# Block-product operands summed in place from twelve staged parts, with a retimed spectral chain, in a gated spectral/GEGLU kernel

## The chip, the cores and the metric

The kernel runs on one core of one Trainium2 chip. The metric is the device time of one execution in microseconds; a profiled execution also gives its span, from the first instruction to the last, which is a little shorter.

## The reference, cut to what matters

```python
x = A_x                                        # [1, 2048, 576], float32
g = sigmoid((x * gate_w).sum(-1, keepdims=True))
X = rfft2(x, axes=(-2, -1)) * (w_r + 1j * w_i) # 2048 x 289 complex filter
a = irfft2(X, s=(2048, 576), axes=(-2, -1))
h = gelu(B_x @ w_gate) * (B_x @ w_up)          # 576 -> 4608, tanh form of gelu
b = h @ w_down                                 # 4608 -> 576
return g * a + (1 - g) * b
```

`B_x` has the same values as `x`. Two unequal halves: a gated feed-forward network, nearly all of the arithmetic, and a two-dimensional FFT filter.

## The kernel before, in words

**Matrix work (TensorE, PE).** Operands are kept as two reduced-precision pieces, high and low, so that a float32 product is three matmuls (high·high, low·high, high·low). The 4608 hidden features are 36 blocks of 128; two blocks for one half of the tokens (1024, as two groups of 512) are a *pair*. There are 36 pairs, q = 0 to 35, the first 18 for one token half, the rest for the other. `PLAN` (L33) says for each pair how its gate and up projections are made:

- `c`, `conv` (L1248): plain chains, 8 of 14 matmuls of 512 columns, 112 in all (`chain`, L755).
- `s`, `products` (L1048): a block-product scheme in which seven products of quarter blocks stand for eight, 7 times 2 times 7 = 98 matmuls (`seven`, L1035). It needs seven operands of x: the quarters a11, a12, a22 and four sums s1 to s4 of the quarters, and as many of the weights, made on ScalarE (ACT) and VectorE (DVE) by `prep_b` and `total`.

The plan before is 2 c, 10 s, 11 c, 13 s. So block products run in two stages, each opened by `operands(p)` (L941), which makes the seven operands of that token half. The quarters come from memory as three feature parts of four quarters each (`load_xs`, L937: two parts before the stage, the third into the place of the first once it is used). Per part: four sums on DVE (L962), copies to the high pieces on ACT (`copy`, L214), differences to the low pieces on DVE (L974), and for the third, packed part the same three steps for seven operands (`tail_of`, L916). They are written to `sx`, which shares its place with the spectral tile buffer `til`, and s4 to `gu[2]`, one of three weight buffers that `conv` rotates through. `operands` waits until the pair before the stage has begun (L954).

Behind each pair stand 8 down projections (`down`, L850), each 12 matmuls of 288 columns, an eviction on ACT (L860) and an accumulating DMA on the POOL queue (L848). `pop` takes them from a list; the first pair of a block-product stage has only 4 to take, at the products that `downs` (L1080) names.

**Spectral work (DVE, ACT, a little PE).** One generator, `spectral` (L600), issues it in a fixed order: operands of stage one; forward FFT along rows for each token half (`forward_rows`); a wait for the first c pair after stage one (`until(2)`); then row-to-tile copies (`into_tiles`, `moved`, L500), the token-axis stages (`first_tiles`; `columns`, L232, with 192 matmuls of 290 columns, the filter, and small DMAs that swap corners between partitions; `last_tiles`), tile-to-row copies (`into_rows`); operands of stage two; and, once stage two has begun (`until(3)`), the inverse FFT along rows and the adds into the output.

**What orders the work.** Everything is laid out when the program is built; each engine then runs its own instructions in that order and waits on semaphores. After every few matmuls the program calls `gap()` (L656). A gap runs timed jobs (`at`), one job of the list `aux`, and then steps of the spectral generator while a *credit* is above zero. `tick` (L648) adds RATE times the matmuls' nominal time, every DVE job of the matrix part subtracts its nominal cost, and every step of the generator subtracts what it yields. A yield of `None` ends the turn until the next gap. At the gap the credit is cut to at most 1.2. In `columns` each of six steps per block of 128 points charges 5.45/6 and yields `None` (L371). Should the operands not be done when stage two is due, L1288 to L1290 force gaps with no matmul between them until they are.

In both stages x for the second token half is reloaded by `reload_x` (L1242) through three staging places, one feature block in every second gap, around pairs 17 and 18.

Of the kernel before, what the change touches and what calls it, by code (L numbers as in the profile page):

```python
# [13 lines left out]
ALU = mybir.AluOpType  # L14
# [15 lines left out]
RATE = 1.0  # L30
STEP = 6
PAIRS = NT // 2
PLAN = "c" * 2 + "s" * 10 + "c" * 11 + "s" * 13  # L33
# [126 lines left out]
def _build(nc, tc, a):  # L160
    with ExitStack() as ctx:
# [70 lines left out]
        def columns():  # L232
# [77 lines left out]
            for kb in range(18):  # L310
# [18 lines left out]
                for g in range(STEP):  # L329
# [41 lines left out]
                    credit[0] -= 5.45 / STEP if on else 0.0  # L371
# [128 lines left out]
        def moved(at):  # L500

            yield None
            for t in range(8):
                for c in range(2):
                    o, i = at(t, c)
                    if c:
                        vec.tensor_tensor(o, i, sgn, ALU.mult)
# [92 lines left out]
        def spectral(rows):  # L600
            yield from operands(0)
# [314 lines left out]
        def tail_of(o, x):  # L916

            copy(o, x)
            yield 0.0
            vec.tensor_tensor(o, x, f(o), ALU.subtract)  # L920
            yield 0.72
            for q in (0, 64):
                copy(o[q:q + 32], x[q:q + 32])
            yield 0.0

        def tails_of(pairs):

            work = [tail_of(*p) for p in pairs]
            for _ in range(3):
                for w in work:  # L930
                    yield next(w)
                yield None
# [4 lines left out]
        def load_xs(p, i):  # L937
            for q in range(4):
                nc.sync.dma_start(parts_of[i % 2][q], a["xs"][p, q // 2, q % 2][:, i])

        def operands(p):  # L941
# [5 lines left out]
            tails = [sx[:, 6144 + TB * i:6144 + TB * (i + 1)] for i in range(6)] + [s4[:, 2048:2560]]  # L947
# [5 lines left out]
            m = out_rows[3][:, 0:TB]  # L953
            while current[0] < starts[p] - 1:  # L954
                yield None
            for i in range(3):
                a11, a12, a21, a22 = parts_of[i % 2]
                if i == 2:
                    yield from tails_of([(ops[n][2], x) for n, x in (("a11", a11), ("a12", a12), ("a22", a22))])
                for o, x, z, op in ((m, a21, a22, ALU.add), (a21, a11, a21, ALU.subtract),  # L960
                                    (a11, m, a11, ALU.subtract), (a12, a12, a11, ALU.subtract)):
                    vec.tensor_tensor(o, x, z, op)  # L962
                    yield 0.72
                sums = (("s1", m), ("s2", a11), ("s3", a21), ("s4", a12))
                yield None
                if i == 2:
                    yield from tails_of([(ops[n][2], x) for n, x in sums])
                else:
                    for n, x in sums:
                        copy(ops[n][0][:, i], x)  # L970
                    yield None
                    yield None
                    for n, x in sums:
                        vec.tensor_tensor(ops[n][1][:, i], x, f(ops[n][0][:, i]), ALU.subtract)  # L974
                        yield 0.61
                if i == 0:
                    load_xs(p, 2)
# [70 lines left out]
        def products(q):  # L1048
# [31 lines left out]
            downs = (1, 1, 1, 1, 0, 0, 0) if q in starts else (0, 1, 1, 1, 2, 1, 2)  # L1080
# [4 lines left out]
            for n, (name, nd) in enumerate(zip(("a11", "a12", "s2", "s1", "s3", "s4", "a22"), downs)):  # L1085
# [19 lines left out]
                if then == "c":  # L1105
# [4 lines left out]
                    elif n == 5:  # L1110
                        prep_gu(q + 1, 0)
                    elif n == 6:
                        at(2, lambda: prep_gu(q + 1, 1))
# [46 lines left out]
        gu_of, where = {}, [gu[2], gu[0], gu[1]]  # L1160
        for q, m in enumerate(PLAN):
            if m == "s":
# [7 lines left out]
                where, base = [w[k // 2], gu[2], w[1 - k // 2]], 2 * (q + n)  # L1170
# [55 lines left out]
        aux.append(lambda: [load_d(1), load_xs(0, 0), load_xs(0, 1)])  # L1226
# [10 lines left out]
        def load_x(i):  # L1237
            if i < 2 * KT:
                tb, k = divmod(i, KT)
                nc.sync.dma_start(xst[i % 3], a["xt"][1][:, k, tb * TB:(tb + 1) * TB])  # L1240

        def reload_x(tb):  # L1242
            for k in range(KT):
                i = KT * tb + k
                aux.append(lambda i=i, k=k: [prep_x(tb, k, xst[i % 3]), load_x(i + 3)])
                aux.append(lambda: None)
# [111 lines left out]
```

## Time and profile before

| | |
|---|---|
| time, median of 3 runs | 1376.36 us (1374.35 to 1376.40) |
| the profiled execution | 1374.25 us, span 1372.5 us |
| PE busy | 1344.1 us (98% of the span), 7364 matmuls |
| weight loads busy | 1186.9 us (86%) |
| DVE busy | 1142.8 us (83%), 1605 instructions |
| ACT busy | 846.9 us (62%), 1444 instructions |
| POOL busy | 263.2 us (19%) |
| DMA | 227.42 MB, mean 166 GB/s |

A busy share is a mean over stages: PE is busy nearly throughout, and DVE is far busier in the block-product stages than in the c stage. Matmuls are pipelined, so a record of 0.39 us does not say how often one can start; the distance between two starts does. The stretches that follow are named by microseconds from the start of the span: c pairs until 79, stage one of block products until 429, c pairs with the spectral tiles and columns until 887, stage two until the end.

### The profile page before, as it was taken

The page shows a single profiled execution, that of the slowest core. Times are in us where ns is not written, and L with a number is a line of the kernel's source. Part 1 is how long each engine was busy: PE and PEld are TensorE (multiplying, and loading weights), DVE is VectorE, ACT ScalarE, POOL GpSimd, SP SyncE. Part 2 cuts the span into 40 slices and gives each one's busy share as a digit, 9 for nine tenths or more (in the row PEclk, how much of TensorE's full clock was granted, in tenths as well). Part 3 has the DMA queues.
Part 4 walks back from the last instruction along what each step waited for, and adds up shares of the span by engine and source line. Part 5 has one row for each costly group of instructions (what it writes and reads, how often), then busy time and mean ns, then how long its engine had stood idle before and what let it go on. Part 6 is the DMA issues. An engine that isn't in the chain of part 4 may idle for free.

```text
span 1372.5 us, 20070 instructions
## 1 busy us (share of the span) xinstructions
PE 1344.1 (98%) x7364; PEld 1186.9 (86%) x7364; DVE 1142.8 (83%) x1605; ACT 846.9 (62%) x1444; POOL 263.2 (19%) x322
## 2 busy tenths in 40 slices
PE   9998999999999999999999999889999999999998
PEld 7887888888889888889888988767888888888888
DVE  7689999989999768867786587689989779989854
ACT  5585676666674455465665544676676776676682
POOL 0011122221122222122210111211222232222231
PEclk9999999999999999999999999989999999999999
DMA  9465776696667877799987657744666797667797
GB/s 332 163 128 146 148 142 131 130 272 129 126 110 147 195 139 148 181 236 236 265 233 222 132 109 206 173 98 103 130 132 129 134 266 131 135 116 137 138 220 181
DMA packets 102770, 227.42 MB, mean 166 GB/s; under 512 B 12432, under 2 KB 22672, under 8 KB 101776
## 3 DMA queue, kind: packets, MB, share of 16 engines
q0 software_dynamic: 44928, 90.98, 44.1%
q1 hardware_dynamic: 57744, 135.17, 29.7%
q8 instruction: 57, 0.93, 0.3%
q14 instruction: 41, 0.34, 0.1%
HBM read 121.70 MB, written 97.26 MB: 160 GB/s over the span
## 4 chain that ended last, share of the span: by engine, by line
PE 85%; DVE 6%; ACT 4%; DMA 2%; issue 2%; SPq 0%; DVEq 0%; ACTq 0%
PE pdn L835 30%; PE pgu L1041 5%; PE pgu L1043 5%; PE pgu L1042 5%; PE pone L1041 5%; PE pgu L760 5%; PE pgu L762 5%; PE pgu L761 4%; PE pone L1043 4%; PE pone L1042 4%; PE pgu L1044 2%; PE pone L1044 2%; PE pone L760 2%; PE pone L762 2%; PE pone L761 2%
## 5 line engine op out<-in xcount | busy, mean ns | idle before, releaser
L848 POOL DMA_DIRECT2D yd<-stg x264 | 228.9, 868 | 994.2 <-ACT stg L860 861.2
L860 ACT ACTIVATE stg<-pdn,omg 128x576 f32<-128x576 f32 x276 | 203.9, 739 | 278.7 <-PE pdn L835 274.1
L835 PE MATMUL pdn<-dn,hb 128*128 128x288 f32 x2556 | 371.2, 295 | 2.5 <-DVE hb L1065 1.3
L835 PEld LDWEIGHTS pdn<-dn,hb 128*128 128x128 f32 x2556 | 357.8, 189 | 14.3 <-DVE hb L1065 1.8
L214 ACT ACTIVATE gu<-wq 64x256 fp32r<-64x256 f32 (+4 forms) x353 | 228.5, 666 | 101.7 <-DVE gu L1006 90.9
L1006 DVE TENSOR_TENSOR gu<-wq,gu 128x768 fp32r<-128x768 f32 x161 | 153.5, 953 | 18.9 <-ACT gu L214 18.5
L835 PE MATMUL pdn<-dn,hx 128*128 128x288 f32 x876 | 134.2, 295 | 0.2 <-DVE wq L899 0.2
L835 PEld LDWEIGHTS pdn<-dn,hx 128*128 128x128 f32 x876 | 124.9, 189 | 4.1 <-DVE wq L899 0.5
L760 PE MATMUL pgu<-xhi,gu 128*128 128x512 f32 x300 | 117.9, 393 | 0.0
L762 PE MATMUL pgu<-xlo,gu 128*128 128x512 f32 x300 | 117.8, 393 | 0.0
L761 PE MATMUL pgu<-xhi,gu 128*128 128x512 f32 x300 | 117.7, 392 | 0.0
L1023 DVE TENSOR_TENSOR wq<-wq 128x768 f32<-128x768 f32 x92 | 87.7, 953 | 7.9 <-ACT gu L214 7.9
L214 ACT ACTIVATE hb<-gl 128x512 fp32r<-128x512 f32 x66 | 41.4, 627 | 51.4 <-DVE gl L817 51.4
L762 PEld LDWEIGHTS pgu<-xlo,gu 128*128 128x128 f32 x300 | 56.6, 189 | 12.3
L760 PEld LDWEIGHTS pgu<-xhi,gu 128*128 128x128 f32 x300 | 56.8, 189 | 9.9
L761 PEld LDWEIGHTS pgu<-xhi,gu 128*128 128x128 f32 x300 | 56.7, 189 | 9.9
L1044 PE MATMUL pgu<-sx,gu 128*128 128x512 f32 x138 | 54.5, 395 | 6.6 <-ACT sx L214 6.6
L739 DVE TENSOR_TENSOR dn<-wq,dn 128x576 fp32r<-128x576 f32 x72 | 54.2, 753 | 5.0 <-ACT dn L214 5.0
L1041 PE MATMUL pgu<-xhi,gu 128*128 128x512 f32 x140 | 55.6, 397 | 2.5 <-DVE xraw L1077 2.4
L1041 PE MATMUL pgu<-sx,gu 128*128 128x512 f32 x140 | 55.7, 398 | 1.9 <-ACT gl L214 1.9
L1041 PE MATMUL pone<-xhi,gu 128*128 128x512 f32 x136 | 53.5, 394 | 3.7 <-DVE xraw L1077 3.7
L1043 PE MATMUL pgu<-sx,gu 128*128 128x512 f32 x140 | 55.2, 395 | 0.0
(243 smaller groups left out, 2871.2 us busy)
## 6 DMA issues: line engine op xcount, KB each, us to landing
yd<-stg POOLq DMA_DIRECT2D x264, 288.0 KB, 4.9
wq<-ws SPq DMA_DIRECT2D x92, 384.0 KB, 4.2
wq<-wd SPq DMA_DIRECT2D x72, 288.0 KB, 4.6
wq<-wgu SPq DMA_DIRECT2D x24, 640.0 KB, 5.8
colm<-col POOLq DMA_DIRECT2D x32, 256.0 KB, 6.3
tmp<-wf SPq DMA_DIRECT2D x16, 290.0 KB, 5.1
hx<-til SPq DMA_DIRECT2D x64, 72.5 KB, 5.0
til<-hx SPq DMA_DIRECT2D x64, 72.5 KB, 3.7
```

What stands on the lines that cost most here:

```text
L214: act.activation(o, i, AF.Copy)
L760: pe.matmul(ps, w[:, 0, k, c], xhi[tb][:, k], start=k == 0, stop=False)
L761: pe.matmul(ps, w[:, 1, k, c], xhi[tb][:, k], start=False, stop=False)
L762: pe.matmul(ps, w[:, 0, k, c], xlo[tb][:, k], start=False, stop=False)
L835: pe.matmul(ps[half], h[:, l, c], d[:, k, half * HD:(half + 1) * HD], start=part == 0 and n == 0, stop=part == 1 and n == 2)
L848: pl.dma_start(yd[u], o, accum_op=ALU.add)
L860: put(u, lambda o: act.activation(o.rearrange("p (c k) -> p c k", c=2), v[:, :, 0:HD], AF.Copy, scale=omg[:, u:u + 1]), i == 0)
L1006: vec.tensor_tensor(o, x.rearrange("p (c k) -> p c k", c=3), f(w[:, 256:1024]).rearrange("p (c k) -> p c k", c=3), ALU.subtract)
L1041: pe.matmul(ps, hi, xh[:, t], start=start and t == 0, stop=False, skip_group_check=True)
L1042: pe.matmul(ps, lo, xh[:, t], start=False, stop=False, skip_group_check=True)
L1043: pe.matmul(ps, hi, xl[:, t], start=False, stop=False, skip_group_check=True)
L1044: pe.matmul(ps, tl, xt, start=False, stop=stop, skip_group_check=True)
```

## The change

In words, by part:

1. `PLAN` is 2 c, 10 s, 10 c, 14 s: pair 22 becomes a block-product pair, and stage two begins one pair sooner.
2. `RATE` 1.0 to 1.03; the cap on the credit 1.2 to 1.4; a step of `columns` charges 4.9/6 in place of 5.45/6.
3. `moved` yields `None` after every second tile in place of every tile.
4. `operands`: all three parts (twelve quarters) have staging places of their own, loaded together: for stage one by the generator's first step (before: eight of them earlier, by an `aux` job at about 25 us), for stage two right after `columns` (before: after `last_tiles`). The sum s1 is written over a22 and not into a separate place; sums charge 0.61 in place of 0.72. Order: the tails of a11, a12, a22 come first, s1 to s3 before s4, copies on ACT one or two per yield; only the last part waits for the pair before the stage.
5. Weight buffers: which of the three `conv` uses when is turned so that `gu[2]` is free one pair before the stage whatever the number of c pairs, and `prep_gu` of the first c pair after a stage is retimed to match (`early`).
6. The first pair of a stage takes its four down projections at products 3, 5, 6 and 7 in place of 1 to 4.
7. `reload_x` starts with the last feature block and uses gaps 0, 2, 4, 6, 10 of eleven.

```diff
-RATE = 1.0
+RATE = 1.03
-PLAN = "c" * 2 + "s" * 10 + "c" * 11 + "s" * 13
+PLAN = "c"*2+"s"*10+"c"*10+"s"*14
...
-                    credit[0] -= 5.45 / STEP if on else 0.0
+                    credit[0] -= 4.9 / STEP if on else 0.0
...
                     else:
                         copy(o, i)
-                yield None
+                if t % 2:
+                    yield None
...
         def spectral(rows):
+            load_xs(0)
+            for _ in range(3):
+                yield None
             yield from operands(0)
...
             cols[0] = False
+            load_xs(1)
             yield from last_tiles()
-            load_xs(1, 0)
-            load_xs(1, 1)
             yield from into_rows(1)
...
-            credit[0] = min(credit[0], 1.2)
+            credit[0] = min(credit[0], 1.4)
...
         parts_of = [[xraw[:, q] for q in range(4)],
-                    [tmp[:, 1536:2048], tmp[:, 2048:2560], misc[:, 0:TB], misc[:, SW:SW + TB]]]
+                    [tmp[:, 1536:2048], tmp[:, 2048:2560], misc[:, 0:TB], misc[:, SW:SW + TB]],
+                    [tmp[:, 0:512], tmp[:, 512:1024], tmp[:, 1024:1536], out_rows[3][:, 0:TB]]]
...
+            def sums(i):
+                a11, a12, a21, a22 = parts_of[i]
+                for o, x, z, op in ((a22, a21, a22, ALU.add), (a21, a11, a21, ALU.subtract),
+                                    (a11, a22, a11, ALU.subtract), (a12, a12, a11, ALU.subtract)):
                     vec.tensor_tensor(o, x, z, op)
-                    yield 0.72
+                    yield 0.61
+            def steps():
+                raw, most = ("a11", "a12", "a22"), ("s1", "s2", "s3")
+                for n in raw:
+                    high(n, 2)
+                yield from sums(0)
+                for n in most:
+                    high(n, 0)
+                yield from sums(1)
+                for n in raw:
+                    low(n, 2)
+                    quarter(n)
+                    yield 0.61
+                for n in most:
+                    high(n, 1)
+                for n in most:
+                    low(n, 0)
+                    yield 0.61
+                while acts:
+                    yield None
+                yield from sums(2)
+                for n in most:
+                    high(n, 2)
+                for n in most:
+                    low(n, 1)
+                    yield 0.61
+                while acts or current[0] < starts[p] - 1:
+                    yield None
+                for i in range(3):
+                    high("s4", i)
+                for n in most:
+                    low(n, 2)
+                    quarter(n)
+                    yield 0.61
+                while acts:
+                    yield None
+                for i in range(3):
+                    low("s4", i)
+                    yield 0.61
+                quarter("s4")
+                while acts:
+                    yield None
+
+            for v in steps():
+                for _ in range(2 if v is None else 1):
+                    if acts:
+                        acts.pop(0)()
+                yield v
...
-            downs = (1, 1, 1, 1, 0, 0, 0) if q in starts else (0, 1, 1, 1, 2, 1, 2)
+            downs = (0, 0, 1, 0, 1, 1, 1) if q in starts else (0, 1, 1, 1, 2, 1, 2)
...
-                where, base = [w[k // 2], gu[2], w[1 - k // 2]], 2 * (q + n)
+                x, y, base = w[k // 2], w[1 - k // 2], 2 * (q + n)
+                where = ([gu[2], x, y], [x, y, gu[2]], [x, gu[2], y])[c % 3]
+                early[q + n - 1] = c % 3
...
-        aux.append(lambda: [load_d(1), load_xs(0, 0), load_xs(0, 1)])
+        aux.append(lambda: load_d(1))
```

In the new `operands`, `high(n, i)` and `quarter(n)` put ACT copies into the list `acts`, `low(n, i)` issues a DVE difference, and `c` is the number of c pairs that follow the stage.

More of the change, by code (lines that the diff above doesn't have):

```diff
@@ L952, in operands @@
             ops["a22"] = (xhi[1][:, 2:4], xlo[1][:, 2:4], tails[6])
[L953 to L970, printed above, removed]
-                    yield None
-                    yield None
[L973 to L977, printed above, removed]
@@ new lines, in operands, with place_of, high, quarter @@
+            where = {"a11": 0, "a12": 1, "a22": 3, "s1": 3, "s2": 0, "s3": 2, "s4": 1}
+            acts = []
+            def place_of(n, i, l):
+                return ops[n][l][:, i] if i < 2 else ops[n][2]
+            def high(n, i):
+                acts.append(lambda: copy(place_of(n, i, 0), parts_of[i][where[n]]))
+            def quarter(n):
+                for k in (0, 64):
+                    acts.append(lambda k=k: copy(ops[n][2][k:k + 32], parts_of[2][where[n]][k:k + 32]))
+            def low(n, i):
+                x = parts_of[i][where[n]]
+                vec.tensor_tensor(place_of(n, i, 1), x, f(place_of(n, i, 0)), ALU.subtract)
```

45 lines of the change are left out of this document (20 added, 25 removed).

## The prediction

> **What bounds the kernel now.** I read the page first: busy shares, then the chain that ended last.
>
> ```profile
> span 1372.5 us, 20070 instructions
> PE 1344.1 (98%) x7364; PEld 1186.9 (86%) x7364; DVE 1142.8 (83%) x1605; ACT 846.9 (62%) x1444; POOL 263.2 (19%) x322
> ...
> PE 85%; DVE 6%; ACT 4%; DMA 2%; issue 2%; SPq 0%; DVEq 0%; ACTq 0%
> ```
>
> PE bounds the kernel: time goes only with matmuls, or with PE waits. Where those waits lie, the windows show, by stage.
>
> ```profile
> 79.00:125.00 46.00, 41.91 (x206) 34.57 (x205) 41.92 (x65) 32.65 (x58) 4.33 (x6) 0.95 0.52 125
> 160.00:195.00 35.00, 35.00 (x196) 31.05 (x195) 32.96 (x52) 24.11 (x47) 6.90 (x8) 0.95 0.73 146
> 230.00:265.00 35.00, 35.00 (x196) 31.06 (x195) 34.90 (x44) 21.86 (x40) 6.91 (x8) 0.95 0.70 131
> 655.00:702.00 47.00, 44.51 (x251) 39.54 (x249) 35.59 (x58) 30.32 (x54) 11.06 (x16) 0.95 1.03 264
> 870.00:905.00 35.00, 28.32 (x147) 24.39 (x145) 25.63 (x38) 24.26 (x43) 3.48 (x4) 0.86 0.36 75
> 905.00:940.00 35.00, 29.58 (x133) 23.64 (x133) 32.90 (x40) 21.81 (x39) 3.46 (x4) 0.91 0.44 96
> ```
>
> Second column: PE busy, full except at the two openings of block-product stages (79:125, 870:940) and a little in the columns (655:702). To price them I took the first matmul of pairs 2, 3, 4, 5 and of 22, 23, 24, 25, with the matmul before pair 22 and one in pair 23, from the timeline of PE (each from its own short stretch).
>
> ```profile
> 79.20 0.39 PE L1041 MATMUL pone<-xhi,gu 128*128 128x512 f32 x1
> 112.22 0.47 PE L1041 MATMUL pgu<-xhi,gu 128*128 128x512 f32 x1 [0.79 <-DVE xraw L1077]
> 148.40 0.40 PE L1041 MATMUL pone<-xhi,gu 128*128 128x512 f32 x1
> 183.45 0.40 PE L1041 MATMUL pgu<-xhi,gu 128*128 128x512 f32 x1
> 848.40 0.39 PE L767 MATMUL pgu<-xtl,gu 128*128 128x512 f32 x1
> 848.62 0.39 PE L760 MATMUL pgu<-xhi,gu 128*128 128x512 f32 x1
> 886.84 0.39 PE L1041 MATMUL pgu<-xhi,gu 128*128 128x512 f32 x1
> 895.00 0.80 PE L1044 MATMUL pgu<-sx,gu 128*128 128x512 f32 x1 [6.63 <-ACT sx L214]
> 931.29 0.47 PE L1041 MATMUL pone<-xhi,gu 128*128 128x512 f32 x1 [1.11 <-DVE xraw L1077]
> 967.43 0.40 PE L1041 MATMUL pgu<-xhi,gu 128*128 128x512 f32 x1
> ```
>
> A settled block-product pair takes 183.45 - 148.40 = 35.05 us, pair 22 as a c pair 886.84 - 848.62 = 38.22. The pitch at 512 columns is 0.22 to 0.23 us (848.40 to 848.62); 98 of 0.2267 make 22.2, so the 96 narrow ones of a full pair take 12.85. A stage's first pair has 4 down projections in place of 8 and should take 22.2 + 6.4 = 28.6. Stage one: 33.02 and 36.18, lost 4.4 + 1.1 = **5.5 us**. Stage two: 44.45 and 36.14, lost 15.9 + 1.1 = **17.0**. What PE waited for:
>
> ```profile
> PE pgu L1044 <- ACT sx L214: 6.6, 1, 6.6
> PE pone L1041 <- DVE xraw L1077: 3.7, 2, 2.6
> PE pone L276 <- DVE colm L269: 2.8, 1, 2.8
> ```
>
> The longest is the row at 895.00 above, for an operand in sx at the opening of stage two: the operands are late. The others are DVE behind its queue, and one block of the columns. The clock column (0.86, 0.91 against 0.95) says that part of the 17.0 is matmuls run at a lower clock between the waits.
>
> **The change part by part.** *Pair 22 as block products*: 38.22 - 35.05 = **-3.2 us**, 14 wide matmuls fewer. This one is certain.
>
> *Are the operands of stage two in time?* The stage is now due one pair (38 us) sooner. The marks of the spectral chain: pair 12 begins (PE); forward rows are done and the tile copies begin, and later the operands (DVE); the column products from first to last; the operands' last copies (ACT).
>
> ```profile
> 428.82 0.40 PE L760 MATMUL pgu<-xhi,gu 128*128 128x512 f32 x1
> ```
> ```profile
> 452.00 0.71 DVE L507 TENSOR_TENSOR til<-rows,sgn 128x289 f32<-128x289 f32 x1
> 870.67 0.69 DVE L962 TENSOR_TENSOR orow<-xraw 128x512 f32<-128x512 f32 x1
> ```
> ```profile
> L276 PE MATMUL pone<-colm x192: 290/298/404, 565.8 to 780.0; 128*128 128x290 f32 x192
> ```
> ```profile
> 900.92 3.84 ACT L214 ACTIVATE sx<-xraw 32x512 fp32r<-32x512 f32 x6
> ```
>
> The chain ended at 904.8, stage two was due at 886.8: 18 us late. Savings:
> - Forward rows ended 23 us after pair 12 began. A block-product pair earns 98 x 0.2265 + 96 x 0.131 = 34.8 of credit and spends 19.6 on its own DVE jobs (4 x 1.22 + 6 x 0.61 + 11 x 0.88 + 2 x 0.68), leaving 15.2; at RATE 1.03, 16.2, or 7% more. Over some 340 us (452 less pair 2's begin and a reload) that is 22 us. Sooner than pair 12 the chain may not go on: **-22**.
> - Row and tile copies: four passes, four `None` fewer each. A c pair has 24 gaps in 38.22 us, 1.59 each: **-25**. With the copies of `til` waiting for a DMA between two of the passes I keep 20.
> - Columns: 16.5 blocks of six steps, 99 gaps, in 214 us. Less 192 column matmuls at the pitch of the narrow ones (12.85/96 = 0.134), 26 us, and 3 of waits, 185 us hold 116 gaps, so 17 were passed over because credit was below zero. The smaller charge and larger rate save between none and all of them (0 to 27 us): **-10**.
> - The rest of 452 to 871, less 214 of columns and four passes of some 19 each, 130 us, is paced by credit: 3%, **-4**.
> - Operands: the first two thirds now run before the wait; dearest at credit, 12 sums at 0.61 for 0.72: **-1**.
>
> Sum 57, from 904.8 to about 848; due at 848.6 less what stage one gives. So just in time, with perhaps 10 to 20 us to either side. Being slightly late now costs little, since a11, a12, a22 come first and s4, which the sixth product takes, last: the wait of 6.6 at the first product's tail should go. What stays is DVE catching up, as in stage one (5.5). I leave 5 of the 17.0: **-12** (bounds 0, if it is as late as before, and -16).
>
> *Stage one.* The parts are now loaded after the stores of the held tiles, and the tails, from the third part, are the first copies on ACT.
>
> ```profile
> 41.73 2.84 SPq L881 DMA_DIRECT2D yd<-til  x4
> ```
> ```profile
> xraw<-xs SPq DMA_DIRECT2D x16, 256.0 KB, 5.0
> ```
> ```profile
> 47.50 3.18 PE pdn L835 x24
> ...
> 53.88 3.18 PE pdn L835 x24
> ```
> ```profile
> L860 ACT ACTIVATE stg<-pdn,omg 128x576 f32<-128x576 f32 x276 | 203.9, 739 | 278.7 <-PE pdn L835 274.1
> ```
> ```profile
> ACT colm L214 <- DMA til<-hx: 2.8, 1, 2.8
> ```
>
> SP is past those stores at 44.6; twelve issues of 0.5 to 0.7 us (2.84 for four) and 5.0 to land put the last quarter at 56 to 58. In the trace every engine starts its instructions in program order, and the copies stand four gaps after, ahead of the eviction of the second down projection (47.50 to 50.7). PE comes to its fourth at 55.5 and needs that buffer. Three copies of 0.64 (3.84 for six) and an eviction of 0.74 after 56 free it at 58.7: PE waits 3 us (0 if the loads land by 52, 5 if at 58). Queued behind on ACT are gelu and evictions; on DVE the sums wait for part one till about 50, and gated products stand behind them; on SP pair 2's weights stand behind the loads, due 25 us later. **+3**. Against it, ACT's copies are done before the stage and spread one to a yield, and the four projections stand where PE waited for DVE: of the 5.5 I take **-2.5** (+3 to -5: the first weights get 3 us less lead). [...] In the trace of before ACT's longest wait for a DMA is the 2.8 above.
>
> *RATE on DVE.* 3% of 34.8 is 1.04 us more spectral work per block-product pair. The window 230:265 shows DVE busy 34.90 of 35, no room. But two neighbours show that records overlap:
>
> ```profile
> 202.17 1.49 DVE L94 TENSOR_TENSOR rows<-rows 128x1280 f32<-128x1280 f32 x1
> 203.57 0.68 DVE L1077 TENSOR_TENSOR xraw<-xraw,pgu 128x512 f32<-128x512 f32 x1
> ```
>
> The next starts 1.40 after a record of 1.49. With 0.09 hidden in each of 44 to 52 instructions, the room is anywhere from 0 to 4 us per pair. No room costs 1.04 in each of 21 pairs with spectral work, 22 us; full room nothing. I take **+1.5**, nearer to room, since PE waits nowhere at the present load and 160:195 shows 2 us free even by the column. [...]
>
> *Copies two by two.*
>
> ```profile
> L214 ACT ACTIVATE til<-rows 128x289 f32<-128x289 f32 x16 | 11.9, 760 | 0.0
> ```
>
> ACT takes two of these per gap, 1.5 us in 1.59, beside its own work; a backlog of 2 to 3 us per pass, which PE's buffers may just bear: **+0.5** (0 to 3). *Columns*: the waits stay (0, -3 to +5). The sums in place are as many and as wide as before: 0. Stage two's loads move ahead of `last_tiles`: SP holds them till the columns' last DVE jobs free their places, with a c pair's weights behind, which have most of 38 us: 0 (to +2). Weight buffers and the x reload move nothing on PE's path: the first c pair's second weights come later, but two chains of 14 (6.3 us) and eight projections (12.85) cover a copy and a difference of 1280 elements, about 1.5 each by the 1.49 above; uncovered, 3.
>
> Sum: -3.2 - 12 + 3 - 2.5 + 1.5 + 0.5 = **-12.7**, from the profiled 1374.25 to 1361.5. The median of the runs shown stands 2.1 higher, where two of three lie, so the forecast is **1363 us**.
>
> **The rivals.**
> *As late as before.* If the chain gains only the 38 us by which the stage was brought forward, the 17.0 stays: 1363 + 12 = 1375, no change. For it: my sum passes 38 by only 19, and 20 of these rest on the copies and 10 on passed gaps. 0.14.
> *Slower: DVE full in the block-product pairs.* It decides where DVE's real work per pair passes 35.05: 1.04 in 21 pairs, 22 in place of 1.5: 1363 + 20.5 = 1383.5. For it the column 34.90 of 35; against it the start distances. 0.11.
> *Columns held by DMA.* 655:702 shows DMA at 1.03 of 16 engines; steps that come sooner would wait for corner DMAs, say 0.6 us in each of 16 blocks: 1363 + 10 = 1373. 0.08.
> *The columns don't shorten*: operands 10 us late, about half of the former wait back: 1368, inside the forecast's own range.
>
> **How the numbers follow.** Forecast 0.67, own range 1351 (-2.5 more at stage one, none of its +3, -4 at stage two, -3 in the columns) to 1370 (+2 on ACT, +2.5 in the copies, +2.5 on DVE). The range to hold 8 in 10 takes in the first rival: 1350 to 1376. 0.2% is 2.7 us, about what runs can tell: faster below 1373.6. Faster: 0.67, half of the columns' 0.08 and 0.04 of the first rival, 0.75; same: 0.13; slower: 0.12.
>
> **What would show it.** Right: 14 matmuls fewer; stage two's first pair at about 29 to 34 us in place of 44.5, with no wait for sx above 2 us; the granted clock at its opening back to 0.95; the last operand copy within 10 us of the stage's first matmul; a new wait of PE or ACT between 50 and 60. Wrong: pairs 3 to 11 longer than 35.05 (DVE full), column pairs with waits for colm, or operand copies again 15 us into stage two.

## The result, and the profile after

| | before | after |
|---|---|---|
| time, median | 1375.36 us (4 runs, 1372.67 to 1376.40) | 1387.16 us (4 runs, 1382.90 to 1389.34) |
| ratio to before, 95% interval | | 1.0085 [1.0056, 1.0114] |
| profiled execution, span | 1374.25, 1372.5 us | 1382.90, 1381.1 us |

The change made the kernel slower by 0.85%. The forecast was 1363 us, faster, and the measured time lies above its range. The profiled execution of the changed kernel is the fastest of its four, 8.65 us above the profiled one of before where the medians are 11.8 apart; the account below is of the two profiled executions. First the page of the changed kernel, in the same lines as before.

```profile
span 1381.1 us, 20064 instructions
...
PE 1343.0 (97%) x7350; PEld 1182.8 (86%) x7350; DVE 1151.6 (83%) x1620; ACT 848.9 (61%) x1462; POOL 264.8 (19%) x322
...
PE 60%; DVE 22%; issue 6%; ACT 6%; DMA 5%; SPq 1%; DVEq 0%; ACTq 0%
```

PE has its 14 matmuls fewer. But the chain of work that ended last goes through DVE for 22% of the span, where it was 6%: PE now waits where it did not. The windows view, in the stretches of the prediction and one more in stage two (second column PE busy, fourth DVE busy):

```profile
79.00:125.00 46.00, 44.05 (x221) 37.22 (x220) 43.28 (x66) 31.76 (x57) 6.56 (x7) 1.00 0.61 136
230.00:265.00 35.00, 35.00 (x196) 31.04 (x195) 34.90 (x42) 21.44 (x39) 6.93 (x8) 1.00 0.68 130
655.00:702.00 47.00, 43.66 (x247) 38.30 (x246) 33.93 (x56) 26.79 (x48) 10.06 (x14) 1.00 1.04 264
870.00:905.00 35.00, 35.00 (x175) 29.78 (x174) 32.54 (x40) 22.04 (x39) 3.46 (x4) 1.00 0.52 107
905.00:940.00 35.00, 35.00 (x195) 31.06 (x194) 34.90 (x42) 21.25 (x37) 6.96 (x8) 1.00 0.64 124
1150.00:1185.00 35.00, 32.68 (x167) 28.45 (x166) 32.37 (x50) 23.69 (x47) 6.93 (x8) 0.95 0.67 123
```

Both openings of block-product stages are better: the second, at 870, has no idle PE at all. What was won there was lost inside stage one, in the columns (655:702) and late in stage two (1150:1185). The same view with the first matmul of a pair as the edge of each stretch makes the first column the length of the pair, beside the 35.05 of a settled one; here pairs 8, 9, 11, 29 and 30:

```profile
289.50:332.20 42.70, 36.97 (x197) 32.09 (x196) 35.20 (x55) 18.91 (x33) 6.62 (x8) 0.96 0.75 168
332.20:368.60 36.40, 35.94 (x196) 31.01 (x196) 36.26 (x46) 21.39 (x39) 6.98 (x8) 1.00 0.68 127
405.60:444.10 38.50, 35.55 (x197) 31.12 (x195) 37.96 (x44) 21.95 (x39) 6.96 (x8) 1.00 0.63 125
1112.00:1148.60 36.60, 35.55 (x195) 31.04 (x195) 36.06 (x43) 21.64 (x39) 6.96 (x8) 1.00 0.66 125
1148.60:1188.00 39.40, 37.08 (x196) 32.59 (x195) 36.37 (x56) 26.80 (x54) 6.93 (x8) 0.96 0.63 115
```

Two kinds of loss stand side by side. In pairs 9, 11 and 29 DVE is busy for all but 0.1 to 0.5 us of a pair that is longer than PE needs: DVE's work is the length of the pair. In pair 8 DVE is idle for 7.5 us and in pair 30 for 3.0, so something else held it there. The waits of PE, and two of the other engines' rows, name the parties (total us, times, longest):

```profile
PE pdn L838 <- ACT stg L863: 6.4, 4, 3.1
PE pgu L1075 <- DVE xraw L1163: 5.7, 1, 5.7
PE pgu L763 <- DVE gl L820: 4.8, 2, 2.9
...
ACT gu L214 <- DVE gu L1040: 175.4, 103, 4.2
...
DVE wq L1057 <- DMA wq<-ws: 10.4, 1, 10.4
...
DVE til L94 <- DMA til<-hx: 6.7, 2, 3.4
```

```profile
ACT gu L214 <- DVE gu L1006: 90.9, 73, 5.9
```

The second fence is the kernel before: ACT's waits for DVE's weight differences have nearly doubled, from 90.9 to 175.4 us (98.9 in e2, the changed kernel at the old pace), so at the new pace ACT too stands behind DVE for longer.

**Where the time went.** The table takes the first matmul of every pair from the trace and gives the time from one to the next less what the pair needs: 38.2 for a c pair, 35.05 for a block-product pair, 28.6 for the first of a stage, 44.6 for the first c pair after one; from the ten or eleven c pairs together 25.7 for the column matmuls is taken off too. All in us.

| kernel | pair 1 | stage one, opening | pair 8 | pairs 9 to 11 | columns | stage two, opening | rest of stage two |
|---|---|---|---|---|---|---|---|
| before | 0.0 | 5.5 | 0.0 | 0.0 | 5.6 | 17.0 | 1.4 |
| after | 3.6 | 2.6 | 7.6 | 6.8 | 12.3 | 0.2 | 8.3 |
| e1_pool_reload | 4.4 | 1.2 | 8.4 | 6.3 | 13.9 | 0.2 | 8.1 |
| e2_old_rate | 1.4 | 1.2 | 0.0 | 0.0 | 5.9 | 33.4 | 1.5 |
| e3_before_rate | 0.0 | 9.3 | 8.4 | 6.8 | 7.8 | 8.5 | 4.5 |
| e4_tails_first | 5.8 | 1.1 | 9.2 | 5.6 | 13.6 | 0.2 | 7.3 |
| e5_later_gate | 4.6 | 1.4 | 8.1 | 6.6 | 16.5 | 0.2 | 8.3 |
| e6_sixteen_turns | 4.2 | 1.4 | 6.8 | 3.1 | 7.8 | 7.8 | 6.0 |
| e7_old_plan_old_rate | 4.1 | 1.2 | 0.0 | 0.0 | 3.4 | 10.7 | 1.4 |
| e8_old_rate_stage_two | 4.8 | 1.2 | 8.2 | 6.4 | 9.7 | 0.2 | 0.0 |
| e9_pool_and_turns | 5.0 | 1.2 | 5.3 | 4.5 | 7.3 | 6.6 | 5.7 |
| e10_rate_in_columns | 4.6 | 1.2 | 0.0 | 0.0 | 13.1 | 0.2 | 0.0 |
| e12_later_operands | 0.0 | 4.7 | 0.0 | 0.0 | 10.4 | 0.2 | 0.0 |
| e13_store_after_blocks | 4.7 | 1.2 | 0.0 | 4.6 | 7.8 | 7.4 | 6.1 |
| e14_old_rate_later_operands | 0.0 | 7.3 | 0.0 | 0.0 | 3.5 | 9.7 | 1.4 |
| e15_mended | 0.0 | 4.7 | 0.0 | 4.2 | 7.6 | 8.0 | 1.4 |

From before to after: +3.6 - 2.9 + 7.6 + 6.8 + 6.7 - 16.8 + 6.9, with -3.2 for pair 22 and +0.3 in pair 0, make +9.0; the spans differ by 8.6.

### The profile page after: what moved, and what is told of

Its sections match the earlier page's. It is cut to its first block, busy times and chain, and to the rows that moved or that the text cites. A ratio compares the mean times of both kernels' runs of the same rounds, so it can differ in the third digit from the quotient of the medians.

```text
span 1381.1 us, 20064 instructions
## 1 busy us (share of the span) xinstructions
PE 1343.0 (97%) x7350; PEld 1182.8 (86%) x7350; DVE 1151.6 (83%) x1620; ACT 848.9 (61%) x1462; POOL 264.8 (19%) x322
## 4 chain that ended last, share of the span: by engine, by line
PE 60%; DVE 22%; issue 6%; ACT 6%; DMA 5%; SPq 1%; DVEq 0%; ACTq 0%
PE pdn L838 21%; PE pgu L763 3%; PE pgu L765 3%; PE pgu L764 3%; DVE gu L1040 3%; PE pone L1075 3%; PE pone L1077 3%; PE pgu L1075 3%; PE pone L1076 3%; PE pgu L1077 3%; PE pgu L1076 3%; DVE wq L1057 2%; PE pone L1078 2%; PE pgu L1078 2%; DVE xraw L1111 1%
## 5 line engine op out<-in xcount | busy, mean ns | idle before, releaser
L838 PE MATMUL pdn<-dn,hb 128*128 128x288 f32 x2472 | 362.2, 296 | 6.6 <-ACT stg L863 6.3
L838 PEld LDWEIGHTS pdn<-dn,hb 128*128 128x128 f32 x2472 | 348.1, 189 | 19.0 <-ACT stg L863 7.3
L214 ACT ACTIVATE gu<-wq 64x256 fp32r<-64x256 f32 (+4 forms) x365 | 235.1, 664 | 195.2 <-DVE gu L1040 175.4
L838 PE MATMUL pdn<-dn,hx 128*128 128x288 f32 x960 | 148.3, 295 | 1.7 <-DVE hx L1099 1.5
L838 PEld LDWEIGHTS pdn<-dn,hx 128*128 128x128 f32 x960 | 136.8, 188 | 6.4 <-DVE hx L1099 2.2
L763 PE MATMUL pgu<-xhi,gu 128*128 128x512 f32 x280 | 109.7, 392 | 7.5 <-DVE gl L820 4.8
L765 PE MATMUL pgu<-xlo,gu 128*128 128x512 f32 x280 | 109.4, 391 | 0.0
L764 PE MATMUL pgu<-xhi,gu 128*128 128x512 f32 x280 | 109.3, 390 | 0.0
L1057 DVE TENSOR_TENSOR wq<-wq 128x768 f32<-128x768 f32 x96 | 91.4, 952 | 20.9 <-ACT gu L214 10.5
L763 PEld LDWEIGHTS pgu<-xhi,gu 128*128 128x128 f32 x280 | 52.6, 188 | 17.6 <-DVE gl L820 5.6
L1075 PE MATMUL pgu<-xhi,gu 128*128 128x512 f32 x144 | 57.0, 396 | 5.7 <-DVE xraw L1163 5.7
L765 PEld LDWEIGHTS pgu<-xlo,gu 128*128 128x128 f32 x280 | 52.5, 188 | 11.4
L764 PEld LDWEIGHTS pgu<-xhi,gu 128*128 128x128 f32 x280 | 52.6, 188 | 9.1
L1075 PE MATMUL pone<-sx,gu 128*128 128x512 f32 x144 | 56.9, 395 | 2.9 <-ACT gl L214 2.6
L1075 PE MATMUL pgu<-sx,gu 128*128 128x512 f32 x144 | 56.7, 394 | 1.3 <-ACT gl L214 1.3
L1077 PE MATMUL pgu<-xlo,gu 128*128 128x512 f32 x144 | 56.6, 393 | 0.0
L1076 PE MATMUL pgu<-sx,gu 128*128 128x512 f32 x144 | 56.4, 392 | 0.2
```

Source lines behind the costliest of these rows:

```text
L214: act.activation(o, i, AF.Copy)
L763: pe.matmul(ps, w[:, 0, k, c], xhi[tb][:, k], start=k == 0, stop=False)
L764: pe.matmul(ps, w[:, 1, k, c], xhi[tb][:, k], start=False, stop=False)
L765: pe.matmul(ps, w[:, 0, k, c], xlo[tb][:, k], start=False, stop=False)
L838: pe.matmul(ps[half], h[:, l, c], d[:, k, half * HD:(half + 1) * HD], start=part == 0 and n == 0, stop=part == 1 and n == 2)
L1057: at(lead, lambda: vec.tensor_tensor(o, u, v, ALU.subtract))
```

## The experiments

"Pace" stands for RATE and the cap on the credit together (1.0 and 1.2 the old, 1.03 and 1.4 the new); no run changes one without the other, so what each of them does alone is not shown. The theory after the comparison: block-product pairs have no DVE time to spare, so the new pace pushes PE into waits; and the faster chain meets a new collision at the row reload in pair 8. The rivals are told with each run.

**The old pace in the changed kernel.**

```diff
-RATE = 1.03
+RATE = 1.0
-            credit[0] = min(credit[0], 1.4)
+            credit[0] = min(credit[0], 1.2)
```

> The changed kernel with RATE 1.0 and the cap of 1.2, the rest as changed. Theory B: pairs 9 to 11 and pairs 27 to 30 (8.3 us over 35.05 each) go back to 35.05, 12 to 20 us less, unless the operands of stage two come late, which gives up to 10 back. Theory A: what is lost depends on where the reload and the corners fall; stage two keeps most of its 8.3 us, and the time moves by less than 6 either way.

Measured 1384.64 us, ratio to before 1.0064 [1.0045, 1.0083]. Stage one falls from 17.0 lost to 1.2, the columns from 12.3 to 5.9, the inside of stage two from 8.3 to 1.5. All of it comes back at one place, the opening of stage two:

```profile
PE pone L1078 <- ACT sx L214: 21.2, 1, 21.2
PE pone L1075 <- ACT gl L214: 8.3, 2, 7.4
```

So the pace is what costs the time inside the stages, and it is also what brings the operands in time: with the old one 33.4 us are lost at the opening of stage two, with the new one 0.2.

**The new pace in the kernel before.** The same two edits the other way, on the kernel before.

> The kernel before with RATE 1.03 and the cap of 1.4 alone. Theory B: block-product pairs with spectral work exceed 35.05 us in both stages, 10 to 20 us lost there, with some 5 to 10 won at the opening of stage two: 0 to 15 us slower than before. Theory A: pairs stay at 35.05 save one at the reload; the opening of stage two is earlier supplied: 5 to 12 us faster than before, or as much slower as a reload on SP costs (7 to 14).

Measured 1393.84 us, 1.0128 [1.0106, 1.0149], the slowest of all and 18 us slower than before, more than the 0 to 15 of theory B. Pairs 8 to 11 lose 8.4 and 6.8 us, where the changed kernel loses 7.6 and 6.8, with none of its other parts present: those losses belong to the pace alone.

**The old plan and the old pace in the changed kernel**, so that only the staged operands, the copies two by two, the shorter column charge and the buffers remain:

```diff
-RATE = 1.03
-PLAN = "c"*2+"s"*10+"c"*10+"s"*14
+RATE = 1.0
+PLAN = "c"*2+"s"*10+"c"*11+"s"*13
-            credit[0] = min(credit[0], 1.4)
+            credit[0] = min(credit[0], 1.2)
```

> The changed kernel with the plan of before (11 c, 13 s), RATE 1.0 and the cap of 1.2. In the run with the old rate alone the operands of stage two came about 38 us late; one c pair more is 38 us. If lateness is what that stage's opening costs, it loses 0 to 5 us here (17.0 before), stage one 1 to 2 (5.6 before), pair 1 some 1 to 3 for the staged loads: 14 to 20 us faster than before, 1356 to 1362. If the opening costs something of its own, 10 us or more stay there and the time is 1366 to 1372.

Measured 1365.37 us, 0.9921 [0.9900, 0.9943]: faster than both kernels, though above the 1356 to 1362 expected. Against e2 (1384.64), whose only difference is the plan, the extra block-product pair at the old pace costs 19 us in place of the 3.2 that it saves: the operands are due 38 us sooner, and 33.4 in place of 10.7 us are lost at the opening. The 10.7 that remain here were expected at 0 to 5, a miss:

```profile
PE pgu L1075 <- ACT gl L214: 5.8, 1, 5.8
PE pdn L838 <- ACT stg L863: 3.4, 2, 2.3
```

ACT has the last operand copies, from 894.02 to 897.84, and 1.58 us of weight copies in front of the eviction at 899.35 that PE waits for in the first pair of the stage.

**The old pace from stage two on**, where the chain has no more operands to bring in time:

```diff
-            credit[0] += RATE * us
+            credit[0] += (1.0 if phase[0] == 3 else RATE) * us
-            credit[0] = min(credit[0], 1.4)
+            credit[0] = min(credit[0], 1.2 if phase[0] == 3 else 1.4)
```

> The changed kernel with RATE 1.0 and the cap of 1.2 from the opening of stage two on. Theory B: pairs 27 to 30 (8.3 us over) fall to 1 to 2 us over, everything ahead stays: 6 to 8 us less than the changed kernel. Theory A: those pairs lose to DMAs and ScalarE whatever the rate: 0 to 3 us less.

Measured 1378.75 us, 1.0019 [1.0004, 1.0033], 8.4 us less than the changed kernel where theory B expected 6 to 8. The rest of stage two falls from 8.3 to 0.0. The program ahead of stage two is that of the changed kernel, so its 4.8 for 3.6 in pair 1 and 9.7 for 12.3 in the columns show how far single profiles scatter. The stretch that showed PE at 32.68 of 35 in the changed kernel:

```profile
1150.00:1185.00 35.00, 35.00 (x195) 31.05 (x195) 34.03 (x48) 24.56 (x46) 6.91 (x8) 1.00 0.68 130
```

So the pace in stage two is the cause there. That a full DVE is the whole way in which it acts is not shown. Of the 8.3 us, pair 27 loses 2.3 with DVE idle for 12.5 and ACT busy for 34.56 of 37.4. Pairs 29 and 30 lose 1.6 and 4.4 just behind a stop of DVE at the second reload of rows (`rows<-bw`), and in pair 30 PE waits for ACT:

```profile
1081.27 1.49 DVE L94 TENSOR_TENSOR tmp<-rows 128x1280 f32<-128x1280 f32 x1 [5.21 <-DMA rows<-bw]
...
1173.66 3.25 PE L838 MATMUL pdn<-dn,hb 128*128 128x288 f32 x12 [2.31 <-ACT stg L863]
```

This stop is 5.0 to 5.8 us in all eight kernels that have the new pace in stage two, and 0.5 to 2.2 in the kernel before, e2, e7, e8, e10 and e12, which have the old one there. No run takes it away at the new pace, so its share stays open.

**Pair 8: whose wait is it?** The timeline of the changed kernel around its start at 289.5 (start, duration, then in brackets the idle time before and what ended it):

```profile
274.50 0.33 SPq L607 DMA_DIRECT2D fw<-rows  x1
284.08 0.33 SPq L575 DMA_DIRECT2D rows<-xn  x1
284.51 0.38 SPq L1025 DMA_DIRECT2D wq<-ws  x1
...
296.49 0.96 DVE L1057 TENSOR_TENSOR wq<-wq 128x768 f32<-128x768 f32 x1 [10.38 <-DMA wq<-ws]
297.48 0.84 ACT L214 ACTIVATE gu<-wq 128x768 fp32r<-128x768 f32 x1 [8.14 <-DVE wq L1057]
300.13 0.63 ACT L214 ACTIVATE hb<-xraw 128x512 fp32r<-128x512 f32 x1 [1.18 <-DVE xraw L1163]
300.15 0.79 PE L1075 MATMUL pgu<-xhi,gu 128*128 128x512 f32 x1 [5.73 <-DVE xraw L1163]
```

The store of the finished rows and the load of the next ones into the same place stand one behind the other on SP. The load's issue waits 9.6 us for the store, and a weight block's load stands behind it. Once issued it takes another 12.0 us to land, where the median of its line is 4.0. DVE stops for that block, ACT for DVE, PE for both. First the pair of transfers was taken to POOL's queue:

```diff
-            nc.sync.dma_start(fw, rows)
+            pl.dma_start(fw, rows)
...
-            load_rows(rows, 1)
+            pl.dma_start(rows[:, 0:8 * D], a["xn"][1])
+            pl.memset(rows[:, 8 * D:], 0.0)
```

> The changed kernel with the store of the forward rows and the reload of the second token half on the POOL queue in place of SP. Theory A (a collision): SP holds pair 8's weight loads behind the reload, which waits 9 us for the store; VectorE starts 10 us behind and stays behind to pair 11. Then pair 8 falls from 42.7 to 35-36 us and pairs 9 to 11 from 36.4-38.4 to 35-36: 10 to 14 us less than the changed kernel. Theory B (VectorE is full by RATE 1.03 and the cap of 1.4): pair 8 falls by up to 7.6, but pairs 9 to 11 keep 1.4 to 3.4 us each: 4 to 8 us less.

Measured 1384.12 us, 1.0058 [1.0037, 1.0079], and pair 8 still loses 8.4:

```profile
297.29 0.69 DVE L426 TENSOR_TENSOR tmp<-rows 128x512 f32<-128x512 f32 x1 [10.65 <-DMA rows<-xn]
```

The theory of the SP queue alone falls: with the block in time, DVE walks into the rows themselves. The generator passes nine empty turns behind the reload; the next theory is that at the new pace fewer gaps are skipped, so that nine turns go by before the rows are there. Sixteen in place of nine, on SP as before:

```diff
             load_rows(rows, 1)
-            for _ in range(9):
+            for _ in range(16):
```

> The changed kernel with 16 empty turns in place of 9 between the reload of the rows and their first use. Theory (nine turns pass in less than the 22 us that store and reload take, since more credit passes over fewer gaps): VectorE's wait of 10 us at 286 goes and pair 8 falls from 42.7 to 35.05-36. Theory A' (pairs 9 to 11 are its aftermath) has these fall from 36.4-38.4 to 35.05 too, 12 to 16 us less in all; theory B (VectorE is full) keeps 1.4 to 3.4 us in each: 6 to 9 us less.

Measured 1378.74 us, 1.0023 [1.0011, 1.0036]; pair 8 loses 6.8, now again by the block's load:

```profile
296.00 0.96 DVE L1057 TENSOR_TENSOR wq<-wq 128x768 f32<-128x768 f32 x1 [10.36 <-DMA wq<-ws]
```

Two waits side by side, then; each edit alone left the other. Both together:

> The changed kernel with both edits at the row reload: store and reload on POOL's queue, and sixteen empty turns in place of nine. Theory (two waits side by side: the block load held 9.6 us behind the store on SP's queue, and the row side step itself reaching the rows too early; each edit alone left the other in place, 8.4 and 6.8 us lost in pair 8): with both gone pair 8 loses under 1.5 us, stage one falls from 17.0 to 8 to 10, and the time is 1374 to 1378. Rival (VectorE is full there whatever it waits for, the waits only show where): pair 8 or the next three lose the same 7 us, time 1379 to 1384.

Measured 1380.17 us, 1.0032 [1.0021, 1.0044], a time that the rival had, and pair 8 at 5.3, where the theory said under 1.5. It failed again, in a way that tells:

```profile
290.39 0.57 POOL L609 DMA_DIRECT2D rows<-xn  x1 [10.54 <-DMA fw<-rows]
...
301.12 0.74 ACT L864 ACTIVATE stg<-pdn,omg 128x576 f32<-128x576 f32 x1 [8.41 <-DMA yd<-stg]
...
303.65 0.50 PE L1076 MATMUL pone<-sx,gu 128*128 128x512 f32 x1 [3.43 <-ACT gl L214]
```

Now POOL is held 10.5 us, the accumulating stores of the down projections stand behind, and ACT has no free staging buffer. Each of the two queues is closed for about 10 us by the two transfers, SP for 9.6 in the changed kernel and POOL for 10.5 here. So the last edit leaves them on SP and changes their place among the block loads:

```diff
+            for _ in range(4):
+                yield None
             nc.sync.dma_start(fw, rows)
             rows = rows_tile()
             load_rows(rows, 1)
-            for _ in range(9):
+            for _ in range(12):
```

> The changed kernel with the row store moved four empty turns later on SP's queue, and twelve turns in place of nine behind the reload. Theory (the store came ahead of the pair's fourth block load, and whichever queue holds the pair of transfers for 10 us stops what is behind it: SP the block load, POOL the sums of yd; at RATE 1.0 the store came after the fourth load and cost nothing): the fourth load is issued before the store, pair 8 loses 0 to 2 us, stage one falls from 17.0 to 8 to 11; the chain is seven turns later, so stage two opens 3 to 8 us late, and the time is 1374 to 1381. Rival (VectorE at its limit makes the loss, the order on the queue does not matter): pair 8 and the three after it still lose 12 us or more.

Measured 1374.69 us, 0.9996 [0.9985, 1.0008]: level with the kernel before. Pair 8 loses nothing, stage one 5.8 in all (expected 8 to 11).

```profile
264.36 8.77 SPq L1027 DMA_DIRECT2D wq<-ws  x4
...
275.96 0.43 SPq L609 DMA_DIRECT2D fw<-rows  x1
287.33 0.33 SPq L575 DMA_DIRECT2D rows<-xn  x1
...
297.79 0.69 DVE L426 TENSOR_TENSOR tmp<-rows 128x512 f32<-128x512 f32 x1 [1.36 <-DMA rows<-xn]
```

All four block loads of the pair are out before the store. SP is closed just as long (11.4 us), with nothing urgent behind. The kernel before had this order as well, its store at 279.58 and its rows at 301.62 after a wait of 0.63: its clean pair 8 was a matter of timing, which the new pace undid.

The 4.6 us that pairs 9 to 11 still lose without the stop agree with a sum over pairs 8 to 11 of the changed kernel (first column length, fourth DVE busy):

```profile
289.50:444.10 154.60, 144.01 (x779) 125.33 (x777) 144.95 (x197) 87.46 (x159) 27.51 (x32) 0.99 0.68 137
```

Four settled pairs have 140.2 us and DVE's work is 144.95, so about 4.8 of the 14.4 lost are work that does not fit, and 9.7 are time in which DVE stood idle.

**Pair 1: the order of the staged loads.** The part whose copies ACT takes first is loaded first:

```diff
-            for i in range(3):
+            for i in (2, 0, 1):
```

> The changed kernel with the third part of the staged operands loaded first. Theory (ScalarE in order): the copies of the tails no longer wait for the last four loads, so the wait of 3.1 us of TensorE for an eviction at 58.8 goes and pair 1 falls from 41.8 to 38.2-38.8: about 3 us less. Rival (the sums of part one then wait four loads longer on VectorE): the wait goes from ScalarE to VectorE and pair 1 keeps 40 us or more.

Measured 1384.84 us, 1.0067 [1.0050, 1.0085]. The rival held: ACT's wait of 5.0 us is gone, and DVE has one for the first part, whose loads now stand behind those of the third; pair 1 grows from 41.8 to 44.0 us.

```profile
54.74 2.87 DVE L962 TENSOR_TENSOR xraw<-xraw 128x512 f32<-128x512 f32 x4 [6.60 <-DMA xraw<-xs]
```

**Columns: the side steps later.** In the changed kernel the inverse steps beside the columns come to the tiles before the corner transfers have landed (the two waits of DVE for `til<-hx` above). They are let go later:

```diff
-                    while gone[0] < (4 * d + 5) * STEP + 5:
+                    while gone[0] < (4 * d + 6) * STEP + 2:
```

> The changed kernel with the inverse tile steps beside the columns let go three column steps later. Theory (they meet corner DMAs that have not landed): VectorE's two waits of 3.4 us for til<-hx go, and with them TensorE's 2 and 3 us at 621 and 670: 4 to 5 us less than the changed kernel, c pairs together at 7 to 8 us over in place of 12.3. Rival (the DMA queues are full there and any order waits): the waits move to other column steps and the time stays within 2 us.

Measured 1388.54 us, 1.0093 [1.0075, 1.0111]. Pairs 16 and 17 fall from 9.8 and 9.3 to 5.9 and 6.5, and pair 21 loses 7.1 in their place. The two waits for `til<-hx` are gone, but in pair 21 DVE now stands 8.8 us for a store of rows (`bw<-rows`): the loss moved, to another transfer than the rival had in mind.

**Looking for a version better than e7.** First e7 with RATE 1.03 and the ceiling 1.4 in c pairs only:

```diff
-            credit[0] += RATE * us
+            credit[0] += (1.03 if PLAN[current[0]] == "c" else 1.0) * us
-            credit[0] = min(credit[0], 1.4)
+            credit[0] = min(credit[0], 1.4 if PLAN[current[0]] == "c" else 1.2)
```

> Eleven column pairs as before, RATE 1.03 and ceiling 1.4 in column pairs alone, 1.0 and 1.2 in block-product pairs. Theory (block-product pairs have no VectorE time to give away, column pairs have a little; the opening of 10.7 us in stage two that was left with the old plan and the old rate comes from a side chain late by about that): the opening falls to 0 to 4, columns cost 3 to 8 where they cost 3.4, stage one stays at 1 to 2, and the time is 1356 to 1363. Rival (the faster pace only runs the chain into waits for the corner's transfers, as in the changed kernel, where columns cost 12.3): columns cost 10 to 12, the opening 4 to 8, time 1365 to 1370.

Measured 1368.34 us, 0.9952 [0.9934, 0.9970]. The opening falls from 10.7 to 0.2 as the theory had it, and the columns rise from 3.4 to 13.1 as the rival had it; the sum is unchanged. Then the same with eight empty turns ahead of the first operand copies:

```diff
             load_xs(0)
-            for _ in range(3):
+            for _ in range(8):
```

> The kernel of the run before (eleven column pairs, faster pace in column pairs alone), with eight empty turns in place of three between the staged loads of stage one and the first copy out of them. Theory (ScalarE reaches the copies before the transfers have landed and holds PE for 3 us in pair 1): pair 1 falls from 42 to 39 or less, the opening of stage one grows by 0 to 2, the rest is as in the run before, so 1 to 3.5 us less than that one. Rival (five turns later the operands themselves are late for stage one): pair 1 falls as much, the opening of stage one grows by 3 to 6, no gain or a loss of up to 3 us.

Measured 1366.13 us, 0.9935 [0.9920, 0.9950]. Pair 1 loses nothing any more, and the opening of stage one 4.7 in place of 1.2: more than the theory's 0 to 2, as the rival had it, and 2.2 us less than e10 by the medians all the same, with intervals that overlap. The same turns at the old pace:

> Eleven column pairs and RATE 1.0 with ceiling 1.2 everywhere, with eight empty turns in place of three ahead of the first copies. Theory (waits of pair 1 go, and what the chain loses is added to the openings): pair 1 falls from 42.3 to 38.5, stage one opens 3 to 5 late where it was 1.2, stage two 11 to 15 late where it was 10.7, time 1364 to 1368, no different from three turns. Rival (the turns cost the chain nothing): 1360 to 1363.

Measured 1367.89 us, 0.9948 [0.9933, 0.9963]: 4.1 won in pair 1, 6.1 lost at the opening of stage one, which is 7.3 late where 3 to 5 were expected.

Last, the changed kernel with its ten-pair plan and the mends of e13, e8 and e12 together:

> The changed kernel with ten column pairs kept and four mends: store four turns later, twelve turns behind the reload, eight turns ahead of the first copies, RATE 1.0 and ceiling 1.2 from stage two on. Theory (each mend takes away its own loss, 7 in pair 8, 3 in pair 1, 8 in stage two, and the chain's delay of about 12 turns opens stage two 5 to 12 late): 1368 to 1374. Rival (waits only move: what is won at one place is lost in the columns and the opening): 1376 to 1381.

Measured 1368.03 us, 0.9946 [0.9926, 0.9966], at the lower end of what the theory had. The intervals of e7, e10, e12, e14 and e15 overlap: mended, the ten-pair plan is about as good as the eleven-pair plan, and none beats e7 by these runs.

## Why the prediction was wrong, by its own steps

**Pair 22, -3.2.** Right for PE's work: 7350 matmuls for 7364. What it costs at the old pace to have the operands 38 us sooner stands in e2 beside e7, 19 us.

**Opening of stage two, -12.** The wait went as forecast, and more: 17.0 lost before, 0.2 after, so -16.8, just past the bound of -16. That the pace would bring much of this is borne out by e2, which loses 33.4 here. ACT's last operand copies in the changed kernel:

```profile
856.25 2.54 ACT L214 ACTIVATE sx<-tmp 32x512 fp32r<-32x512 f32 x4
...
859.58 1.27 ACT L214 ACTIVATE gu<-tmp 32x512 fp32r<-32x512 f32 x2 [0.17 <-DVE gu L956]
```

They end at 860.9, the forecast had 848. That nothing is left of the wait is in part luck, for PE was late itself: stage two began at 870.6, where the forecast had 848.6 less what stage one gives. What 860.9 would have cost against 848.6 is not shown.

**Staged loads in stage one, +3.** Right in mechanism, place and size:

```profile
55.65 1.21 ACT L214 ACTIVATE sx<-tmp 128x512 fp32r<-128x512 f32 x2 [5.01 <-DMA tmp<-xs]
57.53 0.63 ACT L214 ACTIVATE sx<-orow 128x512 fp32r<-128x512 f32 x1 [0.68 <-DMA orow<-xs]
58.07 0.72 ACT L863 ACTIVATE stg<-pdn,omg 128x576 f32<-128x576 f32 x1
...
58.84 1.84 PE L838 MATMUL pdn<-dn,hb 128*128 128x288 f32 x12 [3.12 <-ACT stg L863]
```

The forecast had PE released at 58.7 after 3 us. In the trace the eviction starts on ACT at 58.07, behind the three copies that waited 5.01 and 0.68 us for their loads, and PE's wait for it is 3.12 us.

**Opening of stage one, -2.5.** Right: 5.5 to 2.6.

**RATE on DVE, +1.5.** This is the step that failed. It read 34.90 busy of 35, saw that neighbouring records overlap by 0.09, and took 44 to 52 times 0.09 off as room, "nearer to room". The groups of DVE in that window of the kernel before, first and last of 20:

```profile
L1006 DVE TENSOR_TENSOR gu<-wq,gu 128x768 fp32r<-128x768 f32 x8 | 7.6, 954 | 0.0
...
L685 DVE DVE_READ_ACCUMULATOR misc<-misc,orow 128x1 f32 x1 | 0.1, 88 | 0.0
```

Added up, the 20 groups make 39.6 us (about 1 of it lies beyond the edges) in a window of 35, while the windows column says 34.90. The column counts time in which any record runs, so the overlap was already out of it, and the step took it out twice. The idle time that it left was 0.10 us in 35. The start distance of 1.40 beside the record of 1.49 shows an overlap of 0.09 between two neighbours and says nothing of the room, and "nearer to room" did not hold.

Nor was the room nil. Over pairs 3 to 11 the kernel before has DVE busy for 303.74 of 316.60 us, so 1.4 us free per pair where the new pace asked for 1.04, unevenly spread. Pairs 4 to 7 and 23 to 26 lose nothing at the new pace. The losses begin in pair 8, where DVE stops behind the transfers of rows, and in stage two in pair 27, where ACT is nearly full, and go on behind the second reload; with so little room the time that DVE stood was not made up. Measured: 6.8 in pairs 9 to 11 and 6.9 more than before in stage two, 13.7 us. The rival "DVE full", given 0.11, comes nearest, but its mechanism held in part and its place did not: it had 1.04 in each of 21 pairs. That its 1383.5 lies within 4 us of the measured 1387.16 is in part luck, since it had neither the waits for the rows nor the 6.7 in the columns, nor the 4.8 more that the opening of stage two gave. Nor does any step price the cap of 1.4, which was part of the pace.

So a second piece was in none of the steps: the 7.6 of pair 8. The step counted RATE's price on DVE alone and not what a faster chain meets on SP, a transfer of 2560 KB with another behind it; e13, which moves the two, has pair 8 at 0.0. The prediction knew of "a reload" in this stretch and passed it by.

**Copies two by two, +0.5.** The first c pair lost 1.4; fair.

**Columns, 0 (-3 to +5).** Measured +5.3 beside that 1.4, just over its upper end, and +6.7 in all (by e8's profile of the same program there, 2.6 less). The rival "columns held by DMA" had the mechanism: DVE waited for the corner transfers twice, 3.33 and 3.41 us, each time with a wait of PE for DVE right behind, 1.91 us at 621.07 and 2.86 at 670.10.

```profile
619.65 0.76 DVE L94 TENSOR_TENSOR til<-til 128x580 f32<-128x580 f32 x1 [3.33 <-DMA til<-hx]
```

With the pace taken back (e2) the columns stand at 5.9, as before. So the price of the pace was 7.6 + 6.8 + 6.9 in block-product pairs and some 4 to 6 in the columns, 25 to 28 us, against the 1.5 taken.

The last sum, 1361.5 and 2.1, is 1363.6 and was put down as 1363; nothing hangs on it. The signs to look for were the right ones: pairs of stage one longer than 35.05 stood in the list of what would prove the forecast wrong, and that is what the profile showed.

## What to carry to other kernels

A busy column of 34.9 in 35 leaves 0.1 of room, however much the records overlap: here they add up to 39.6, and the overlap is already out of the column. Take the room over a whole stage and not from one window, and ask what the faster work will meet: here a room of 1.4 us per pair, on average enough for the 1.04 asked, did not make up a wait of 10.4 us. So raise the pace of work that fills gaps only in the stages that have gaps, and end it where nothing is due any more. A store and a load that waits for it closed their queue for the store here, SP for 9.6 us and POOL for 10.5; what helped was a place where nothing urgent stands behind, not the other queue.

## What the runs showed of the hardware

A load into the place that a 2560 KB store reads waited for the store, with the next transfers of its queue behind it: 9.6 us on SP (274.50 to 284.08), 10.5 on POOL in e9, 11.4 on SP in e13, and 22 us passed from the store's issue to the first use of the new rows (275.96 to 297.79 in e13). And the granted clock in the windows did not always move the pace: 230:265 shows 0.95 in the kernel before and 1.00 in the changed one, with 196 matmuls in both. Much lower values went with a slower pace: in the kernel before, behind the wait of 6.63 us that ends at 895.00, the matmuls of 512 columns start 0.43 us apart (six distances from 895.59 to 898.15) where they start 0.22 apart at 848.40, and 895:915 shows 0.80. That bears out the prediction's reading of 0.86 and 0.91.
